# Both expert products and the transposes as two 64-row halves that exchange PSUM banks half way

## The chip, the cores and the metric

One core of a Trainium2 chip. The metric is the device time of one execution in microseconds (us), median of several executions. Everything is fp32. "Faster" and "slower" mean a difference of more than 2%.

## The reference, cut to what matters

Eight sequences of 3584 tokens with 192 channels pass a causal convolution of seven taps (softmaxed weights per head), then a layer of eight experts. Each token goes to one expert, either its own best or, when a locality gate says so, the expert of the token before it:

```python
logits = np.einsum('bsd,de->bse', x, w_gate)
local_gate = 1.0 / (1.0 + np.exp(-np.einsum('bsd,de->bse', x, w_local).squeeze(-1)))
for b in range(B):
    prev_e = -1
    for s in range(S):
        fresh_e = int(np.argmax(logits[b, s]))
        e = fresh_e if s == 0 or local_gate[b, s] < 0.5 else prev_e   # (cut)
        prev_e = e
        # p = softmax(logits[b, s])
        h = np.maximum(x[b, s] @ w1[e], 0.0)      # 192 -> 1024
        out[b, s] = p[e] * (h @ w2[e])            # 1024 -> 192
```

## The kernel before

The kernel convolves and routes the tokens in 16 groups of 14 x 128 and writes each token to a slot of its expert. Slots come in units of 128 tokens. The expert layer then runs over *blocks* of one unit (57 of them) or two units (87) of one expert; routing of later groups is put between the blocks as "side work". The constants: `P = 128`, `D = 192`, `DR = 64` (the rest of 192 over 128), `F = 1024`, `FK = 8` slices of 128 hidden features, `KT = 2` units at most, `BT = 256` tokens.

192 input channels do not fill 128 rows evenly. The first product therefore has eight full-array matmuls (channels 0 to 127), and eight 64-row matmuls for channels 128 to 191, of which two run side by side, one on each half of the rows, in different PSUM banks. So the array changes between 64-row and 128-row mode twice in every block.

```python
# PSUM, 8 banks: bg (2, side work), xps (1), hps (4), yps (1)

def turn(n, xg):                       # the next block's tokens, transposed
    xps = xps_p.tile([P, 2, BT], F32, name="xps")
    for d in range(2):
        for k in range(n):
            nc.tensor.transpose(xps[:, d, k * P:(k + 1) * P],
                                xg[:, k, Y0 + d * P:Y0 + (d + 1) * P], identity=ident)
    xT = tp.tile([P, 2, BT], F32, name="xT")
    nc.vector.tensor_copy(xT[:, :, :n * P], xps[:, :, :n * P])
    return xT

def hidden(n, wb, xT):                 # first product
    # ... hT, hps (four banks), w = slice(0, n * P)
    for half in range(2):
        for j in range(2):
            for row in range(2):
                rows = slice(row * DR, (row + 1) * DR)
                f0 = F + (half * 2 + j) * P
                nc.tensor.matmul(hps[half * 2 + row][:, j, w], lhsT=wb[rows, f0:f0 + P],
                                 rhs=xT[rows, 1, w], start=(j == 0), stop=False,
                                 skip_group_check=True)
    for s in range(FK):
        nc.tensor.matmul(hps[s // 2][:, s % 2, w], lhsT=wb[:, s * P:(s + 1) * P],
                         rhs=xT[:, 0, w], start=False, stop=True, skip_group_check=True)
        if s % 2:
            nc.scalar.activation(hT[:, s - 1:s + 1, w], hps[s // 2][:, :, w], Act.Relu)
    return hT

def output(n, wb, xg, hT):             # second product, scaled by the gate, scattered
    yps = yps_p.tile([P, KT, D], F32, name="yps")
    for k in range(n):
        for m in range(FK):
            nc.tensor.matmul(yps[:, k, :], lhsT=hT[:, m, k * P:(k + 1) * P],
                             rhs=wb[:, WA + m * D:WA + (m + 1) * D],
                             start=(m == 0), stop=(m == FK - 1))
    # ... ScalarE scales yps into o_sb, GpSimd scatters the rows

for i, (_, n, _, _) in enumerate(blocks):
    # ... loads of later blocks
    hT = hidden(n, wbs[i], xT)
    if i + 1 < len(blocks):
        xT = turn(blocks[i + 1][1], xgs[i + 1])
    step(2.1 * n, 1)                   # side work
    output(n, wbs.pop(i), xgs.pop(i), hT)
    step(2.1 * n, n)
```

The next block's transposes stand between the two products. TensorE does them while ScalarE drains the last bank of the first product.

Of the kernel before, what the change touches and what calls it, by code (L numbers as in the profile page):

```python
# [8 lines left out]
F32 = mybir.dt.float32  # L9
I32 = mybir.dt.int32  # L10
Act = mybir.ActivationFunctionType
Alu = mybir.AluOpType
# [5 lines left out]
P = 128  # L18
# [64 lines left out]
def kernel(  # L83
# [19 lines left out]
    op = ctx.enter_context(tc.tile_pool(name="op", bufs=2))  # L103
    bg_p = ctx.enter_context(tc.tile_pool(name="bg_p", bufs=2, space=PSUM))
    xps_p = ctx.enter_context(tc.tile_pool(name="xps_p", bufs=1, space=PSUM))
# [19 lines left out]
    with tc.tile_pool(name="scr", bufs=1) as scr:  # L125
        w = scr.tile([1, H, KC], F32, name="w")
        nc.scalar.dma_start(out=w, in_=weight.rearrange("(o h) k -> o h k", o=1))
        x_in = {0: load_x(0)}
        nc.gpsimd.memset(ones, 1.0)
        any_ = scr.tile([1, 1], F32, name="any_")  # L130
        nc.scalar.activation(any_, ones[:1, :1], Act.Exp)
        make_identity(nc, ident)
        taps(nc, scr, w)
        cps = bg_p.tile([P, GQ * P], F32, name="bg")
        nc.tensor.matmul(cps[:, :H * KC], lhsT=ones[:1, :], rhs=w.rearrange("o h k -> o (h k)"),
                         start=True, stop=True)
        nc.vector.tensor_copy(c.rearrange("p h k -> p (h k)"), cps[:, :H * KC])
# [24 lines left out]
    def conv(g, x_sb, on_pe=(), alone=False):  # L162
# [16 lines left out]
        def others():  # L179
            for i, h in enumerate(on_pe):  # L180
                cps = hps_p.tile([P, 2, BT], F32, name="hps")
                acc = cps.rearrange("p a b -> p (a b)")[:, :NT * GS]
                for k in range(KC):
                    nc.tensor.matmul(acc, lhsT=dg_of(i, k), rhs=chans(h, k),  # L184
                                     start=(k == 0), stop=(k == KC - 1))
                    if k == KC - 1:
                        nc.scalar.copy(cols(h), acc.rearrange("p (t d) -> p t d", d=GS))
                    yield
# [69 lines left out]
    tabi = {}  # L258



    def route(g, alone):
# [8 lines left out]


        yT = yt.tile([P, 3, 4, 2 * P], F32, name="yT")
        for u in range(3):
            for jj in range(0, 4, 2):
                tps = (hps_p.tile([P, 2, BT], F32, name="hps") if alone and u else
                       bg_p.tile([P, 2, 2 * P], F32, name="bg"))
                for j in range(2):
                    for q in range(GQ):
                        t = min(2 * (4 * q + jj + j), NT - 2)  # L280
                        src = (yr[:, t:t + 2, :].rearrange("p t d -> p (t d)") if u == 2
                               else y_sb[:, t + u, Y0:Y0 + P])
                        nc.tensor.transpose(tps[:, j, q * P:(q + 1) * P], src, identity=ident)  # L283
                if alone and g == 0 and jj:
                    nc.vector.tensor_copy(yT[:, u, jj:jj + 2, :], tps)  # L285
                else:
                    nc.scalar.copy(yT[:, u, jj:jj + 2, :], tps)  # L287
            if not alone:
                yield "hop"
        lps = bg_p.tile([P, 2 * P], F32, name="bg")  # L290
        for u in range(3):
# [9 lines left out]
        yield "hop"  # L301
        ltp = bg_p.tile([P, GQ * P], F32, name="bg")
        for q in range(GQ):
            nc.tensor.transpose(ltp[:, q * P:(q + 1) * P], lsb[:, q * P:(q + 1) * P],  # L304
                                identity=ident)
        yield "pe"
        lt = sm.tile([P, NT + 2, E + 1], F32, name="lt")
        nc.vector.tensor_copy(
            lt.rearrange("p (q j u) e -> p q j (u e)", q=GQ, u=2),
            ltp.rearrange("p (q j e) -> p q j e", q=GQ, j=4)[:, :, :, :2 * (E + 1)])  # L310
        yield 0.3
        lg = lt[:, :NT, :E]
# [34 lines left out]

        rps = bg_p.tile([P, GQ * P], F32, name="bg")
        nc.tensor.transpose(rps[:1, :P], run[:, NT - 1:NT], identity=ident)
# [3 lines left out]
        else:  # L353
            nc.vector.memset(so_far[:, 0:1], 0.0)
        yield 0.1
        yield "pe"
        krow = sm.tile([1, P], F32, name="krow")
        nc.vector.tensor_copy(krow, rps[:1, P:2 * P])
        yield 0.2
        nc.vector.tensor_tensor_scan(so_far[:, 1:], krow, rps[:1, :P], so_far[:, 0:1],  # L360
                                     Alu.mult, Alu.add)
        yield 0.4
        yield "hop"
        bps = bg_p.tile([P, GQ * P], F32, name="bg")
        nc.tensor.transpose(bps[:, 0:1], so_far[:, :P], identity=ident[:1, :1])
        rs = sm.tile([P, NT], F32, name="rs")
        nc.vector.tensor_reduce(rs, ex, axis=AX.X, op=Alu.add)
# [5 lines left out]
        yield "pe"  # L373
        before = sm.tile([P, 1], F32, name="before")
        nc.vector.tensor_copy(before, bps[:, 0:1])
        yield 0.2
        nc.vector.tensor_tensor_scan(run, nf, ch, before, Alu.mult, Alu.add)
# [14 lines left out]
        yield "hop"  # L392
        nps = bg_p.tile([P, GQ * P], F32, name="bg")
        nc.tensor.matmul(nps[:, :E], lhsT=tri, rhs=mine, start=True, stop=True)
        nc.tensor.matmul(nps[:, E:2 * E], lhsT=ones, rhs=mine, start=True, stop=True)  # L395
        offs = sm.tile([P, E], F32, name="offs")
        nc.vector.tensor_tensor(offs, base, less, op=Alu.subtract)
# [27 lines left out]
        yield 0.2  # L425
        yield "placed"
        nc.vector.tensor_tensor(base, base, nps[:, E:2 * E], op=Alu.add)
        yield 0.2
        was = g - 1 if g else None
        if ONE[g] > (ONE[was] if g else 0):  # L430
# [143 lines left out]
    def load_rows(i):  # L574
# [16 lines left out]
        return xg  # L591

    def turn(n, xg):

        xps = xps_p.tile([P, 2, BT], F32, name="xps")
        for d in range(2):
            for k in range(n):
                nc.tensor.transpose(xps[:, d, k * P:(k + 1) * P],  # L598
                                    xg[:, k, Y0 + d * P:Y0 + (d + 1) * P], identity=ident)
        xT = tp.tile([P, 2, BT], F32, name="xT")  # L600
        nc.vector.tensor_copy(xT[:, :, :n * P], xps[:, :, :n * P])  # L601
        return xT

    def hidden(n, wb, xT):
        hT = hp.tile([P, FK, BT], F32, name="hT")
        hps = [hps_p.tile([P, 2, BT], F32, name="hps") for q in range(FK // 2)]
        w = slice(0, n * P)


        for half in range(2):  # L610
            for j in range(2):
                for row in range(2):
                    rows = slice(row * DR, (row + 1) * DR)
                    f0 = F + (half * 2 + j) * P
                    nc.tensor.matmul(hps[half * 2 + row][:, j, w], lhsT=wb[rows, f0:f0 + P],  # L615
                                     rhs=xT[rows, 1, w], start=(j == 0), stop=False,
                                     skip_group_check=True)
        for s in range(FK):
            nc.tensor.matmul(hps[s // 2][:, s % 2, w], lhsT=wb[:, s * P:(s + 1) * P],  # L619
                             rhs=xT[:, 0, w], start=False, stop=True, skip_group_check=True)  # L620
            if s % 2:
                nc.scalar.activation(hT[:, s - 1:s + 1, w], hps[s // 2][:, :, w], Act.Relu)  # L622
        return hT

    def output(n, wb, xg, hT):
        yps = yps_p.tile([P, KT, D], F32, name="yps")
        for k in range(n):
            for m in range(FK):
                nc.tensor.matmul(yps[:, k, :], lhsT=hT[:, m, k * P:(k + 1) * P],  # L629
                                 rhs=wb[:, WA + m * D:WA + (m + 1) * D],  # L630
                                 start=(m == 0), stop=(m == FK - 1))
        o_sb = op.tile([P, KT, D], F32, name="o_sb")
        for k in range(n):
            gate = xg[:, k, 0:1]
            nc.scalar.activation(o_sb[:, k, :], yps[:, k, :], Act.Copy, scale=gate)  # L635

# [115 lines left out]
    for i, (_, n, _, _) in enumerate(blocks):  # L752
        ensure(i)
        weights(i + AHEAD)
        hT = hidden(n, wbs[i], xT)
        if i + 1 < len(blocks):
            xT = turn(blocks[i + 1][1], xgs[i + 1])
        step(2.1 * n, 1)
        output(n, wbs.pop(i), xgs.pop(i), hT)
        step(2.1 * n, n)  # L760


def _w1_layout(np, w1):


    rest = w1[:, P:, :].reshape(E, DR, 2, 2, 2, P)
    rest = rest.transpose(0, 3, 1, 2, 4, 5).reshape(E, P, F // 2)
    return np.concatenate([w1[:, :P, :], rest], 2)
# [36 lines left out]
```

## Time and profile before

| before | |
|---|---|
| median of 3 executions | 1467.62 us |
| TensorE busy, granted clock | 98% of the span, full |
| ScalarE, VectorE, GpSimd busy | 35%, 44%, 34% |
| period of a block of two units, no side work beside it | 11.217 us |
| period of a block of one unit, the same | 5.894 us |
| first block starts | 69.7 us |

The *period* is the distance between the starts of the first product in consecutive blocks, late in the run where the routing is finished. 144 blocks with few varieties make up 1312 of 1466 us, so a term of 0.1 us in every block is 14 us, 1%. A timeline row is read as start, duration, engine, line, operation, output and inputs, count, and in brackets how long the engine had been idle and what ended that. The page's lines and two timelines are shown in the prediction below.

### The profile page before, as it was taken

How to read it: one execution, taken by the hardware profiler on the slowest of the kernel's cores; microseconds unless marked ns; L12 is line 12 of the kernel's file. 1: busy time of each engine (PE TensorE's matmuls, PEld its weight loads, DVE VectorE, ACT ScalarE, POOL GpSimd, SP SyncE). 2: the span in 40 equal slices, each digit the busy share in tenths (PEclk: the TensorE clock that was granted, in tenths of full speed). 3: DMA queues.
4: the chain of work that ended last, by engine and by line, in shares of the span. 5: the costliest groups of instructions: out<-in, count | busy, mean ns of one | idle time of the engine just before them, and what ended most of it. 6: DMA issues, size and time to landing. Idle time of an engine off the chain costs nothing.

```text
span 1465.7 us, 25910 instructions
## 1 busy us (share of the span) xinstructions
PE 1434.6 (98%) x9792; PEld 1288.0 (88%) x9792; DVE 650.3 (44%) x1756; ACT 512.9 (35%) x1098; POOL 499.5 (34%) x524
## 2 busy tenths in 40 slices
PE   7799999999999999999999999999999999999998
PEld 4598999989888898888988889889889988999997
DVE  7676766676666666666666664220000000000000
ACT  3244444343343433434334343232222222223332
POOL 1442434334344443444434344344121111112111
PEclk9899999999999999999999999999999999999999
DMA  4499989967475675756757556566555455547883
GB/s 166 137 402 358 341 318 388 337 260 271 171 268 202 241 260 188 254 202 239 260 190 255 201 187 209 187 223 218 174 192 195 167 175 196 188 156 255 299 310 119
DMA packets 66414, 343.01 MB, mean 234 GB/s; under 512 B 12656, under 2 KB 23655, under 8 KB 45810
## 3 DMA queue, kind: packets, MB, share of 16 engines
q1 hardware_dynamic: 44064, 288.66, 55.5%
q0 software_dynamic: 22224, 52.70, 9.3%
q8 instruction: 77, 1.26, 0.3%
q14 instruction: 47, 0.39, 0.1%
q10 hardware_dynamic: 2, 0.00, 0.0%
HBM read 288.51 MB, written 53.49 MB: 233 GB/s over the span
## 4 chain that ended last, share of the span: by engine, by line
PE 61%; issue 29%; POOL 6%; DMA 2%; DVE 1%; POOLq 0%; ACT 0%; SPq 0%; DVEq 0%; ACTq 0%
PE yps L629 25%; PE hps L619 17%; PE hps L615 9%; POOL out_dram L638 5%; PE bg L283 3%; PE xps L598 2%; PE hps L184 2%; PE bg L294 2%; POOL slots L450 2%; DVE y_sb L201 1%; DMA xg<-slots 1%; DMA x_sb<-in_x_dram 1%; POOLq L638 0%; PE bg L304 0%; PE bg L395 0%
## 5 line engine op out<-in xcount | busy, mean ns | idle before, releaser
L629 PE MATMUL yps<-wb,hT 128*128 128x192 f32 x3696 | 625.6, 326 | 0.0
L629 PEld LDWEIGHTS yps<-wb,hT 128*128 128x128 f32 x3696 | 597.2, 190 | 0.2
L638 POOL DMA_INDIRECT out_dram<-o_sb,xg x231 | 240.9, 1043 | 830.1 <-ACT o_sb L635 763.2
L619 PE MATMUL hps<-xT,wb 128*128 128x256 f32 (+1 forms) x2304 | 441.5, 345 | 0.0
L619 PEld LDWEIGHTS hps<-xT,wb 128*128 128x128 f32 x2304 | 364.2, 191 | 67.3 <-issue 29.0
L201 DVE SCALAR_TENSOR_TENSOR y_sb<-x_sb,c,y_sb 128x336 f32<-128x336 f32 x720 | 411.1, 581 | 19.5 <-ACT y_sb L177 2.4
L622 ACT ACTIVATE hT<-hps 128x512 f32<-128x512 f32 (+1 forms) x576 | 295.5, 513 | 344.5 <-PE hps L619 337.4
L601 DVE COPY xT<-xps 128x512 f32<-128x512 f32 (+1 forms) x144 | 84.4, 586 | 739.2 <-PE xps L598 739.2
L635 ACT ACTIVATE o_sb<-yps,xg 128x192 f32<-128x192 f32 x231 | 87.8, 418 | 546.4 <-PE yps L629 544.0
L450 POOL DMA_INDIRECT slots<-y_sb,posi x224 | 219.5, 980 | 110.5 <-issue 89.1
L615 PE MATMUL hps<-xT,wb 64*128 64x256 f32 (+1 forms) x2304 | 240.9, 349 | 1.2 <-DVE y_sb L201 0.7
L615 PEld LDWEIGHTS hps<-xT,wb 64*128 64x128 f32 x2304 | 183.4, 188 | 43.4 <-issue 17.2
L598 PE MATMUL xps<-ident,xg 128*128 128x128 f32 x462 | 74.3, 273 | 4.6 <-DMA xg<-slots 4.6
L598 PEld LDWEIGHTS xps<-ident,xg 128*128 128x128 f32 x462 | 57.9, 142 | 13.7 <-DMA xg<-slots 2.7
L177 ACT ACTIVATE y_sb<-x_sb,c 128x336 f32<-128x336 f32 x116 | 65.9, 579 | 0.4
L287 ACT COPY yT<-bg 128x512 f32<-128x512 f32 x87 | 46.6, 590 | 4.9 <-PE bg L283 4.8
L184 PE MATMUL hps<-x_sb,wb 128*128 128x336 f32 x112 | 34.5, 467 | 3.7 <-DMA x_sb<-in_x_dram 3.7
L184 PEld LDWEIGHTS hps<-x_sb,wb 128*128 128x128 f32 x112 | 21.9, 199 | 14.1 <-issue 5.0
L283 PE MATMUL bg<-ident,y_sb 128*128 128x128 f32 x240 | 31.2, 273 | 1.8 <-DVE y_sb L201 0.7
L283 PEld LDWEIGHTS bg<-ident,y_sb 128*128 128x128 f32 x240 | 27.5, 141 | 3.4 <-issue 1.1
L294 PE MATMUL bg<-yT,wg 128*32 128x256 f32 (+1 forms) x384 | 25.0, 358 | 1.3 <-DVE yT L285 1.3
L294 PEld LDWEIGHTS bg<-yT,wg 128*32 128x32 f32 x384 | 12.3, 109 | 9.7 <-issue 3.3
(139 smaller groups left out, 349.5 us busy)
## 6 DMA issues: line engine op xcount, KB each, us to landing
wb<-in_w_dram SPq DMA_DIRECT2D x144, 1536.0 KB
x_sb<-in_x_dram SPq DMA_DIRECT2D x16, 1920.0 KB
xg<-slots SPq DMA_DIRECT2D x87, 258.0 KB
xg<-slots SPq DMA_DIRECT2D x57, 129.0 KB
out_dram<-o_sb,xg POOLq DMA_INDIRECT x231
slots<-y_sb,posi POOLq DMA_INDIRECT x224
slots<-pad SPq DMA_DIRECT2D x1, 129.0 KB
slots<-pad,toi POOLq DMA_INDIRECT x8
```

What stands on the lines that cost most here:

```text
L184: nc.tensor.matmul(acc, lhsT=dg_of(i, k), rhs=chans(h, k), start=(k == 0), stop=(k == KC - 1))
L201: nc.vector.scalar_tensor_tensor(cols(h), chans(h, k), c[:, h, k:k + 1], cols(h), Alu.mult, Alu.add)
L283: nc.tensor.transpose(tps[:, j, q * P:(q + 1) * P], src, identity=ident)
L450: ins = nc.gpsimd.indirect_dma_start(out=slots[:, :], in_=rows, in_offset=None, out_offset=bass.IndirectOffsetOnAxis(ap=to, axis=0)).ins
L598: nc.tensor.transpose(xps[:, d, k * P:(k + 1) * P], xg[:, k, Y0 + d * P:Y0 + (d + 1) * P], identity=ident)
L601: nc.vector.tensor_copy(xT[:, :, :n * P], xps[:, :, :n * P])
L615: nc.tensor.matmul(hps[half * 2 + row][:, j, w], lhsT=wb[rows, f0:f0 + P], rhs=xT[rows, 1, w], start=(j == 0), stop=False, skip_group_chec ...
L619: nc.tensor.matmul(hps[s // 2][:, s % 2, w], lhsT=wb[:, s * P:(s + 1) * P], rhs=xT[:, 0, w], start=False, stop=True, skip_group_check=True)
L622: nc.scalar.activation(hT[:, s - 1:s + 1, w], hps[s // 2][:, :, w], Act.Relu)
L629: nc.tensor.matmul(yps[:, k, :], lhsT=hT[:, m, k * P:(k + 1) * P], rhs=wb[:, WA + m * D:WA + (m + 1) * D], start=(m == 0), stop=(m == FK - 1))
L635: nc.scalar.activation(o_sb[:, k, :], yps[:, k, :], Act.Copy, scale=gate)
L638: sent = nc.gpsimd.indirect_dma_start(out=out, in_=o_sb[:, k, :], in_offset=None, out_offset=bass.IndirectOffsetOnAxis(ap=xg.bitcast(I32)[ ...
```

## The change

The intent: a 64-row pair takes the slot of one full matmul (0.216 us for 256 columns, the prediction's reading), so if *everything* in a block runs in 64-row mode, the array does not change mode there. Each half takes the rows 0 to 63 or 64 to 127 of the contraction. Two row halves must not write one PSUM bank at once (the prediction names the page that says so), so each works on banks of its own and they exchange banks half way. A sequencer-only instruction on ScalarE ("pass") waits for both halves' last matmuls before the exchange and lets the next ones go. The first product no longer interleaves two kinds of matmuls but runs twelve steps (one matmul on each half, two slots of TensorE time). The second product is cut into two parts, and the next block's transposes move from between the products to between these parts. Only blocks of two units exchange banks in the second product; in a block of one unit each half keeps a bank of its own, and VectorE adds the two results at the end. The two banks that side work had for itself are given to the wider `xps` and `yps`, so side work borrows `hps` banks and has to copy its results out earlier.

```diff
+    def turn_half(to, src, half):
+        rows = slice(half * DR, (half + 1) * DR)
+        nc.tensor.transpose(to, src[rows, :], identity=ident[rows, rows])
 ...
     def turn(n, xg):
-        xps = xps_p.tile([P, 2, BT], F32, name="xps")
+        xps = xps_p.tile([P, 2, 512], F32, name="xps")
 ...        (each transpose becomes two of 64 rows, VectorE puts the halves together)
+    ORDER = [[(0, 0), (1, 0), (0, 1), (1, 1), (2, 0), (3, 0), (2, 1), (3, 1),
+              (4, 0), (5, 0), (6, 0), (7, 0)],
+             [(4, 0), (5, 0), (4, 1), (5, 1), (6, 0), (7, 0), (6, 1), (7, 1),
+              (0, 0), (1, 0), (2, 0), (3, 0)]]
+    def pass_by(last_of):
+        seen = nc.scalar.nop()
+        for half in range(2):
+            tc.add_manual_dep(seen.ins, last_of[half], SYNC, reason="the bank's")
+        return seen
     def hidden(n, wb, xT):
 ...
+        for at in range(len(ORDER[0])):
+            for half in range(2):
+                f, last = ORDER[half][at]
+                rows = slice(half * DR, (half + 1) * DR)
+                f0 = F + f % 4 * P if last else f * P
+                b = f // 2
+                mm = nc.tensor.matmul(hps[b][:, f % 2, w], lhsT=wb[rows, f0:f0 + P],
+                                      rhs=xT[rows, last, w], start=(left[b] == 6),
+                                      stop=(left[b] <= 2), skip_group_check=True)
 ...        (waits for the pass at steps 9 and 11)
+            for half in range(2):
+                f, last = ORDER[half][at]
+                b = f // 2
+                left[b] -= 1
+                if not left[b]:
+                    nc.scalar.activation(hT[:, 2 * b:2 * b + 2, w], hps[b][:, :, w], Act.Relu)
-    def output(n, wb, xg, hT):
+    def output(n, wb, hT, yps, part, done):
+        for m in [0, 1, 4, 5, 2, 3, 6, 7]:
+            if n == 1 and (m % 4 < 2) == part:
+                continue
+            for half in range(2):
+                rows = slice(half * DR, (half + 1) * DR)
+                k = (part + half) % 2 if n == KT else 0
 ...        (one 64-row matmul; two units: part 1 waits for the pass)
 ...
         hT = hidden(n, wbs[i], xT)
+        output(n, wbs[i], hT, yps, 0, done)
         if i + 1 < len(blocks):
             xT = turn(blocks[i + 1][1], xgs[i + 1])
         step(2.1 * n, 1)
-        output(n, wbs.pop(i), xgs.pop(i), hT)
+        output(n, wbs.pop(i), hT, yps, 1, done)
+        send(n, xgs.pop(i), yps)
```

In `ORDER` a pair is (feature slice f, rest-of-channels flag); slice f lies in bank f // 2. `ORDER[0]` is the upper half's list, `ORDER[1]` the lower's. Follow a bank and count its six steps: bank 0 gets four from the upper half (steps 1 to 4) and two from the lower (9, 10); bank 2 the reverse; so 0 and 2 are complete after step 10, and 1 and 3 after step 12.

## The prediction

> **What bounds the kernel now.** I read the page first: engine totals, slices, then the costliest groups.
>
> ```profile
> PE 1434.6 (98%) x9792; PEld 1288.0 (88%) x9792; DVE 650.3 (44%) x1756; ACT 512.9 (35%) x1098; POOL 499.5 (34%) x524
> ...
> PEclk9899999999999999999999999999999999999999
> ...
> L629 PE MATMUL yps<-wb,hT 128*128 128x192 f32 x3696 | 625.6, 326 | 0.0
> ...
> L619 PE MATMUL hps<-xT,wb 128*128 128x256 f32 (+1 forms) x2304 | 441.5, 345 | 0.0
> ...
> L622 ACT ACTIVATE hT<-hps 128x512 f32<-128x512 f32 (+1 forms) x576 | 295.5, 513 | 344.5 <-PE hps L619 337.4
> ...
> L615 PE MATMUL hps<-xT,wb 64*128 64x256 f32 (+1 forms) x2304 | 240.9, 349 | 1.2 <-DVE y_sb L201 0.7
> ...
> L598 PE MATMUL xps<-ident,xg 128*128 128x128 f32 x462 | 74.3, 273 | 4.6 <-DMA xg<-slots 4.6
> ```
>
> TensorE is busy 98% of the span at full clock; its four expert lines take 1382 of 1435 us and wait for almost nothing. ScalarE and VectorE are at 35 and 44%. So the time is TensorE's, and any gain must be TensorE slots saved. (Every f32 matmul stands as two instructions; a transpose as one.)
>
> The second view is the timeline of a block of two units (256 tokens) late in the run, where no side work is left:
>
> ```profile
> 1106.23 2.00 PE L615 MATMUL hps<-xT,wb 64*128 64x256 f32 x16
> ...
> 1108.15 3.72 PE L619 MATMUL hps<-xT,wb 128*128 128x256 f32 x16
> 1109.38 0.60 ACT L622 ACTIVATE hT<-hps 128x512 f32<-128x512 f32 x1 [2.31 <-PE hps L619]
> 1110.18 0.60 ACT L622 ACTIVATE hT<-hps 128x512 f32<-128x512 f32 x1 [0.21 <-PE hps L619]
> 1111.05 0.60 ACT L622 ACTIVATE hT<-hps 128x512 f32<-128x512 f32 x1 [0.27 <-PE hps L619]
> ...
> 1111.71 0.60 PE L598 MATMUL xps<-ident,xg 128*128 128x128 f32 x4
> 1111.91 0.60 ACT L622 ACTIVATE hT<-hps 128x512 f32<-128x512 f32 x1 [0.27 <-PE hps L619]
> ...
> 1112.15 5.37 PE L629 MATMUL yps<-wb,hT 128*128 128x192 f32 x32
> ...
> 1117.44 1.60 PEld L615 LDWEIGHTS hps<-xT,wb 64*128 64x128 f32 x16 [0.23 <-issue]
> 1117.44 2.00 PE L615 MATMUL hps<-xT,wb 64*128 64x256 f32 x16
> ```
>
> The period is 11.22 us, the same for 29 such blocks in a row. Steady starts inside a phase lie 0.216 us apart for 256 columns (a pair of 64-row matmuls, which start 7 ns apart, also takes 0.216), 0.1626 for 192 and 0.109 for a transpose. Then 8 pairs x 0.216 = 1.73, 16 x 0.216 = 3.46, 4 x 0.109 = 0.44, 32 x 0.1626 = 5.20: sum 10.82. The missing 0.39 us lies in two places, where the array goes from 128 rows to 64 (1112.15 to 1117.44 is 5.29, not 5.20, and the first pair after it takes 0.320 instead of 0.216) and back (about 0.20 each). Also note that ScalarE drains the first product while it still runs: four evictions, each beginning as a bank completes, the last beside the next block's transposes.
>
> The same view for a block of one unit:
>
> ```profile
> 1331.45 2.05 PE L619 MATMUL hps<-xT,wb 128*128 128x128 f32 x16
> 1332.26 1.66 ACT L622 ACTIVATE hT<-hps 128x256 f32<-128x256 f32 x4 [1.06 <-PE hps L619]
> ...
> 1333.34 0.38 PE L598 MATMUL xps<-ident,xg 128*128 128x128 f32 x2
> ...
> 1333.56 2.77 PE L629 MATMUL yps<-wb,hT 128*128 128x192 f32 x16
> ...
> 1336.25 1.16 PE L615 MATMUL hps<-xT,wb 64*128 64x128 f32 x16
> ```
>
> Period 5.894 us: 24 slots x 0.1117 + 16 x 0.1626 + 2 x 0.109 = 5.50, and again 0.40 for two switches. There are 87 blocks of two units and 57 of one (counts of the xg loads), so 87 x 11.217 + 57 x 5.894 = 1312 us; 70 us pass before the first block, and the remaining 84 us are side work (routing of later groups) put between blocks, 5.17 us a group in the steady part.
>
> **What the Trainium skill says.** "TensorEngine Tiling (Array Packing)", section "Key Properties": changing the tiling mode drains TensorE, while tiles of one mode run independently. The trace agrees: some 0.2 us a switch, two a block, and pairs 7 ns apart. "PSUM — Partial Sum Buffer", section "PSUM bank collisions raise a hardware error": two row tiles may not write one bank at a time, and software must see to it. Hence the exchange of banks; no run yet shows its price. "TensorE: Matmul & The Clock Gate", section "LDWEIGHTS": a load costs its columns at 1.2 GHz (107 ns for 128), whatever the rows. The trace agrees: matmuls with 8 moving columns behind 128-column loads still come 0.112 us apart. A weight load of a transpose, however, lasts 142 ns against 190 for others, so a transpose of half the rows may come faster than 0.109 us a pair.
>
> **The change, part by part.**
>
> (a) Switches. All expert matmuls become 64-row pairs. A pair takes a full matmul's slot, so the slots stay 24 and 32 (24 and 16), and both switches go: -0.39 us x 87 and -0.40 x 57 = -57 us. That is the intent.
>
> (b) Transposes. The two halves move 64 columns instead of 128. If the pair is bound by the 57 ns that a transpose's load takes beyond its fixed 84, estimate 0.064 us a pair instead of 0.109; if by issue or a full load, no gain. Up to -0.18 us a two-unit block, but see (d).
>
> (c) The wait for the evictions, which I take to decide it. Each half begins in banks of its own, and all four banks complete only in the last four of the twelve steps: banks 0 and 2 together after step 10, banks 1 and 3 after step 12. The second product now follows at once; the transposes no longer stand between. By the order of the built instructions, its first matmul waits for the *second* eviction (bank 2 is drained first, the product begins with bank 0). From the start T of the last matmuls of step 10, two units: the eviction begins at T+0.475 (1109.38 less 1108.91, the start of the fourth matmul of L619), the second ends one back-to-back interval later (0.49, from four copies of 512 columns in a row in the opening): T+0.475+0.598+0.49 = 1.56. A ScalarE result lets a weight load start 0.052 us later (seen where the logits are transposed), and the first load without prefetch costs 0.104 more, as at the switches: T+1.72. TensorE arrives at T+5x0.216 = 1.08. Stall 0.64 us. One unit: T+0.372+0.281+0.384+0.156 = 1.19 against 5x0.1117 = 0.56: stall 0.635 us.
>
> (d) The exchange in the second product (two units only). The halves swap columns' banks only after ScalarE has seen the first part end; meanwhile the next transposes run. Matmul end 0.333, ScalarE's pass some 0.065, back to a load 0.05, unprefetched load 0.104: 0.55 after the last start, less its own slot 0.163 = 0.39 us, against 0.26 to 0.44 of transposes. So transposes plus exchange cost 0.39 to 0.44, as the transposes alone do today. The exchange inside the first product has 0.5 us or more of slack and costs nothing.
>
> Bare blocks: two units 24x0.216 + 0.64 + 5.20 + 0.41 = 11.44 (+0.22); one unit 2.68 + 0.635 + 2.60 + 0.13 to 0.22 = 6.09 (+0.20). Over all: 87 x 0.22 + 57 x 0.20 = +31 us.
>
> (e) Side work. Its transposes may gain up to 26 x 0.045 = 1.2 us a group, but the two small full-array groups (carries, counts) now stand alone in 64-row surroundings and pay two switches each, +0.4, the logits and the single-row transpose +0.2 each: about zero to +0.7 us a group. Borrowed banks must be copied out by ScalarE before the first product takes them. They are allotted last, so I see a wait of about 0.3 us only with one-unit blocks. Together +3 us for 14 groups, with the opening.
>
> Sum: 1467.6 + 31 + 3 = about 1501 us.
>
> **Rivals.** First, the intent holds: the evictions hide, the switches go, transposes shorten: 1467.6 - 57 - up to 20 = 1390 to 1410. For it: the 0.39 us a block is real and all engines but TensorE have spare time. Against it: spare share doesn't help when both evictions start within one step of the end; 1.2 us of ScalarE work cannot fit in the 0.86 us of the last two steps. Second, the stall equals the gain: were the first load's 0.104 hidden and the transposes at 0.064 in one-unit blocks, the bare blocks come out at +0.10 and +0.05, giving about 1480. Third, worse: side work on ScalarE (0.48 us a copy or scaling) stands ahead of an eviction or a pass, each delaying TensorE, or the sequencer cannot feed twice the instructions: 1520 to 1540. Against the last: the L615 phase of one-unit blocks sustains four instructions in 0.112 us. Memory is no rival: weights are prefetched three blocks ahead and blocks grow longer.
>
> **Range and chances.** Switch savings and the eviction stall rest on measured intervals (0.05 us of error each, 7 us over 144 blocks); half transposes and side work add some 10. So 1501, range 1480 to 1524. The 2% line is 1497, inside the range but below the middle: slower by over 2% 0.60, within 0.34, faster 0.06.
>
> **What would show it.** Right: late two-unit blocks with a period near 11.44 and one-unit blocks near 6.09; TensorE's weight load of the second product idle about 0.6 us a block with ScalarE's eviction as releaser, and evictions in back-to-back couples at the end of the first product; no 0.32 us first pairs between products. Wrong: no wait for hT, or periods under 11.0 and 5.6 (then the matmuls' real ends are earlier than I read them); or the loss lying in groups with side work alone; or pairs of 192 columns slower than 0.163 us.

## The result, and the profile after

The changed kernel takes 1494.6 us (median, 1494.31 to 1494.98), against 1467.65 of the kernel before beside it: ratio 1.0182, with a 95% interval of 1.0164 to 1.02. It is 1.8% slower, which the 2% rule calls the same (in a second set below, the interval touches 1.02 and the rule says unclear). (Ratios here are the mean time of one kernel's fast runs over that of the other's of the same rounds, so not quite the ratio of the medians quoted.) The result is correct, and the clock was full but for stretches of the opening and the last 3 us.

The changed kernel's page, costliest groups (busy time, mean ns of one, then idle time before them and what ended it):

```profile
PE 1408.2 (94%) x16670; PEld 1272.2 (85%) x16670; DVE 649.0 (43%) x1773; ACT 479.9 (32%) x1168; POOL 500.9 (34%) x524
...
L681 PE MATMUL yps<-wb,hT 64*128 64x192 f32 x7392 | 672.4, 330 | 52.2 <-ACT hT L671 52.2
L681 PEld LDWEIGHTS yps<-wb,hT 64*128 64x128 f32 x7392 | 594.9, 187 | 99.6 <-ACT hT L671 98.1
...
L671 ACT ACTIVATE hT<-hps 128x512 f32<-128x512 f32 (+1 forms) x576 | 248.8, 519 | 422.6 <-PE hps L658 422.6
...
L264 PEld LDWEIGHTS xps<-ident,xg 64*128 64x128 f32 x924 | 52.6, 139 | 2.9 <-DMA xg<-slots 0.3
L264 PE MATMUL xps<-ident,xg 64*128 64x64 f32 x924 | 52.2, 221 | 0.2 <-DMA xg<-slots 0.2
```

TensorE now does *less* busy time (1408 us against 1435) in a longer span. The difference is in the last columns: before, the second product had waited 0.0 us for matmuls and 0.2 for weight loads; now its weight loads wait 98.1 us for ScalarE's evictions. The view of waits counts 144 of them, one for each block, 0.68 us each:

```profile
PEld yps L681 <- ACT hT L671: 98.1, 144, 1.1
```

The timeline of two late blocks of two units:

```profile
1153.32 2.87 PE L681 MATMUL yps<-wb,hT 64*128 64x192 f32 x32 [0.37 <-ACT hT L671]
...
1156.03 0.41 PE L264 MATMUL xps<-ident,xg 64*128 64x64 f32 x8
...
1156.31 2.87 PE L681 MATMUL yps<-wb,hT 64*128 64x192 f32 x32
...
1159.01 5.35 PE L658 MATMUL hps<-xT,wb 64*128 64x256 f32 x48
...
1163.59 2.06 ACT L671 ACTIVATE hT<-hps 128x512 f32<-128x512 f32 x4 [3.63 <-PE hps L658]
1164.72 2.58 PEld L681 LDWEIGHTS yps<-wb,hT 64*128 64x128 f32 x32 [0.77 <-ACT hT L671]
1164.72 2.87 PE L681 MATMUL yps<-wb,hT 64*128 64x192 f32 x32 [0.37 <-ACT hT L671]
```

The period is 1164.72 less 1153.32, 11.40 us. Take it apart by starts:

| stretch | starts | measured | work at full pace | lost |
|---|---|---|---|---|
| first product | 1159.01 to 1164.72 | 5.71 | 24 x 0.216 = 5.18 | 0.53 |
| second product, part one | 1153.32 to 1156.03 | 2.71 | 16 x 0.1626 = 2.60 | 0.11 |
| transposes | 1156.03 to 1156.31 | 0.28 | 4 x 0.063 = 0.25 | 0.03 |
| second product, part two | 1156.31 to 1159.01 | 2.70 | 2.60 | 0.10 |

The four evictions, which before began one by one while the first product ran, are now one row of ScalarE of four back to back: it begins 4.58 us into the product and lasts until after the second product would have started. The second product starts 1.13 us after the first eviction does, which is two evictions (one interval of 0.49 and one duration of 0.60) and a hand-over of 0.05. (The 0.063 is the median distance of pairs of half transposes in this trace. The 0.03 and the 0.10 after it I put down to the exchange; blocks of one unit, which have none, lose 0.06 at that place.) The 0.37 us in TensorE's bracket is smaller than the 0.53 lost between starts, because it counts from the matmuls' modelled ends.

A late block of one unit, same view:

```profile
1401.85 2.84 PE L658 MATMUL hps<-xT,wb 64*128 64x128 f32 x48
...
1404.34 1.21 ACT L671 ACTIVATE hT<-hps 128x256 f32<-128x256 f32 x4 [1.86 <-PE hps L658]
1405.05 1.57 PE L681 MATMUL yps<-wb,hT 64*128 64x192 f32 x16 [0.36 <-ACT hT L671]
...
1406.45 0.29 PE L264 MATMUL xps<-ident,xg 64*128 64x64 f32 x4
...
1407.93 2.85 PE L658 MATMUL hps<-xT,wb 64*128 64x128 f32 x48
```

Its period is 6.08 us: 0.52 us are lost before the second product (3.20 against 24 x 0.1117 = 2.68), and its first part takes 1.40 instead of 1.30.

Where the 27.5 us between the two profiled spans (1493.2 and 1465.7) are:

| | us |
|---|---|
| 87 blocks of two units x (11.405 - 11.217) | +16.4 |
| 57 blocks of one unit x (6.083 - 5.894) | +10.8 |
| first block starts at 73.4 instead of 69.7 us | +3.7 |
| rest: side work between blocks and the end | -3.4 |

The sums of the actual distances between block starts say where the -3.4 lies: the blocks of two units take 15.3 us more than before and not 16.4, those of one unit 7.8 and not 10.8, and from the last block's start to the end it is 0.8 us more. So blocks that have side work beside them pay less for the change than bare ones. (A steady group of five two-unit blocks with side work costs about 5.0 to 5.1 us more than five bare ones; it was 5.17 before.)

The opening is longer for at least two reasons, which no run separates. Its convolution matmuls now write the wide `xps` and `yps` tiles, of which two matmul groups share one, and TensorE waits 0.53 us for ScalarE five times there, once before. And the granted clock was at half from 34.7 to 41.5 us and for 13.7 us from 65.4 on, before only for 10.2 us from 63.3 on; in the first of these stretches six convolution matmuls took 3.73 us instead of 1.86.

### The profile page after: what moved, and what is told of

It is laid out like the page before. It is cut to its first block, busy times and chain, and to the rows that moved or that the text cites. A ratio compares the mean times of both kernels' runs of the same rounds, so it can differ in the third digit from the quotient of the medians.

```text
span 1493.2 us, 40292 instructions
## 1 busy us (share of the span) xinstructions
PE 1408.2 (94%) x16670; PEld 1272.2 (85%) x16670; DVE 649.0 (43%) x1773; ACT 479.9 (32%) x1168; POOL 500.9 (34%) x524
## 4 chain that ended last, share of the span: by engine, by line
PE 54%; issue 30%; ACT 6%; POOL 6%; DVE 3%; DMA 0%; POOLq 0%; DVEq 0%; ACTq 0%
PE yps L681 25%; PE hps L658 22%; ACT hT L671 5%; POOL out_dram L702 5%; PE hps L264 2%; PE hps L308 2%; PE yps L185 1%; POOL slots L467 1%; PE xps L264 1%; PE xps L185 1%; DVE y_sb L202 1%; DMA x_sb<-in_x_dram 0%; DVE xT L624 0%; PE hps L407 0%; POOLq L702 0%
## 5 line engine op out<-in xcount | busy, mean ns | idle before, releaser
L681 PE MATMUL yps<-wb,hT 64*128 64x192 f32 x7392 | 672.4, 330 | 52.2 <-ACT hT L671 52.2
L681 PEld LDWEIGHTS yps<-wb,hT 64*128 64x128 f32 x7392 | 594.9, 187 | 99.6 <-ACT hT L671 98.1
L658 PE MATMUL hps<-xT,wb 64*128 64x256 f32 (+1 forms) x6912 | 636.5, 337 | 1.2 <-DVE xT L627 1.2
L658 PEld LDWEIGHTS hps<-xT,wb 64*128 64x128 f32 x6912 | 563.0, 188 | 51.9 <-DVE y_sb L202 3.7
L671 ACT ACTIVATE hT<-hps 128x512 f32<-128x512 f32 (+1 forms) x576 | 248.8, 519 | 422.6 <-PE hps L658 422.6
L624 DVE COPY xT<-xps 128x512 f32<-128x512 f32 x87 | 60.2, 692 | 592.9 <-PE xps L264 592.9
L301 ACT COPY yT<-hps 128x512 f32<-128x512 f32 x93 | 49.8, 592 | 44.5 <-PE hps L264 44.4
L264 PEld LDWEIGHTS xps<-ident,xg 64*128 64x128 f32 x924 | 52.6, 139 | 2.9 <-DMA xg<-slots 0.3
L264 PE MATMUL xps<-ident,xg 64*128 64x64 f32 x924 | 52.2, 221 | 0.2 <-DMA xg<-slots 0.2
L308 PE MATMUL hps<-yT,wg 128*32 128x256 f32 (+1 forms) x384 | 25.1, 367 | 2.4 <-issue 2.1
```

Source lines behind the costliest of these rows:

```text
L264: nc.tensor.transpose(to, src[rows, :], identity=ident[rows, rows])
L308: nc.tensor.matmul(lps[32 * j:32 * j + 32, :w], lhsT=wg[:, u, :], rhs=yT[:, u, j, :w], start=(u == 0), stop=(u == 2))
L624: nc.vector.tensor_copy(to.rearrange("p h d k s -> p h (d k) s"), xps[:, :, :BT].rearrange("p h (x s) -> p h x s", s=DR))
L658: mm = nc.tensor.matmul(hps[b][:, f % 2, w], lhsT=wb[rows, f0:f0 + P], rhs=xT[rows, last, w], start=(left[b] == 6), stop=(left[b] <= 2), s ...
L671: nc.scalar.activation(hT[:, 2 * b:2 * b + 2, w], hps[b][:, :, w], Act.Relu)
L681: mm = nc.tensor.matmul(yps[:, half if n == 1 else k, :D], lhsT=hT[rows, m, k * P:(k + 1) * P], rhs=wb[rows, WA + m * D:WA + (m + 1) * D], ...
```

## The experiments

Twelve runs of eight kernels were made, in three sets: the first on one chip, the second and third on another. The letters are those of the expectations. Three theories at the start, and two that were added:

- **W (the evictions).** The change saves the switches (0.40 us a block), and gives back more, because two evictions must end between the completion of banks 0 and 2 and the start of the second product. Then an edit that drains in the right order, or completes banks earlier, takes off computable amounts.
- **X (the exchanges)** of banks by way of ScalarE cost the time, and **Y (the pairs themselves)**: half matmuls come slower, or twice the instructions cannot be fed. Under both, the wait for `hT` is only where the cost shows; such edits leave the time at 1494 us or raise it.
- **V (the chip, added after the first set).** That chip, or the state it was in, makes TensorE's semaphore updates late. Its rival **Z**: the edits themselves do.

### Set one, on a slower chip

Four edits of the changed kernel. **e1** lets the second product begin with bank 2, which ScalarE drains first:

```diff
-        for m in [0, 1, 4, 5, 2, 3, 6, 7]:
+        for m in [4, 5, 0, 1, 6, 7, 2, 3]:
 ...
-                                      start=(m == 0 and not part),
-                                      stop=(m == FK - 1 and part == 1), skip_group_check=True)
-                if n == KT and part and m == 0:
+                                      start=(m == 4 and not part),
+                                      stop=(m == 3 and part == 1), skip_group_check=True)
+                if n == KT and part and m == 4:
```

> Only the order in which the second product takes its blocks of hidden units changes: it begins with bank 2, which ScalarE drains first, instead of bank 0. Theory W (the first matmul waits for two evictions in a row): the wait shrinks by the second eviction's interval, 0.49 us with two units and 0.28 with one, to about 0.15 and 0.35 us. Periods 10.92 and 5.80, in all 87 x 0.49 + 57 x 0.28 = 59 us less than the changed kernel: 1436 us. Rival X (the exchange of banks, which goes through ScalarE, is what costs): nothing changes, 1494. Rival Y (half matmuls come slower, or twice the instructions cannot be fed): nothing changes either, 1494.

**e2** leaves the second product alone, and orders the first so that banks 0 and 2 are complete after step 8 of 12 instead of 10:

```diff
-    ORDER = [[(0, 0), (1, 0), (0, 1), (1, 1), (2, 0), (3, 0), (2, 1), (3, 1),
-              (4, 0), (5, 0), (6, 0), (7, 0)],
-             [(4, 0), (5, 0), (4, 1), (5, 1), (6, 0), (7, 0), (6, 1), (7, 1),
-              (0, 0), (1, 0), (2, 0), (3, 0)]]
+    ORDER = [[(0, 0), (1, 0), (0, 1), (1, 1), (6, 0), (7, 0), (4, 0), (5, 0),
+              (2, 0), (3, 0), (2, 1), (3, 1)],
+             [(4, 0), (5, 0), (4, 1), (5, 1), (2, 0), (3, 0), (0, 0), (1, 0),
+              (6, 0), (7, 0), (6, 1), (7, 1)]]
 ...
-            if at in (3, 7):
-                passed[8 if at == 3 else 10] = pass_by(last_of)
+            if at in (3, 5):
+                passed[6 if at == 3 else 8] = pass_by(last_of)
```

> Only the first product's order changes: each half now does 4 steps on its first bank, 2 on the other half's second bank, 2 on the other half's first bank, 4 on its second bank. Banks 0 and 2 are complete after step 8 instead of 10, four steps before the end; the slack of both exchanges is two steps. The second product still begins with bank 0, drained second. Theory W: no wait with two units (eviction done 1.72 us after the start of step 8's last matmuls, TensorE there after 1.94), 0.19 us left with one unit (1.19 against 1.00). Periods 10.77 and 5.64: 87 x 0.64 + 57 x 0.445 = 81 us less, 1414 us. Rival X: the exchanges have less slack than before (one had four steps), so the time rises above 1494. Rival Y: 1494.

**e3** is e2 with the second product in the order in which that first product's banks are drained, `for m in [4, 5, 0, 1, 2, 3, 6, 7]` (flags and wait moved as in e1, with the stop at m == 7).

> Both orders together; the second product takes banks 2, 0, 1, 3, as they are drained. Theory W: no wait for evictions at all, periods 11.405 - 0.64 = 10.77 and 6.083 - 0.635 = 5.45: 87 x 0.64 + 57 x 0.635 = 92 us less than the changed kernel, 1403 us, which is 4.4% faster than the kernel before. Rivals X and Y: 1494 or more.

**e4** puts the next block's transposes back between the products, where they stood before the change:

```diff
-        output(n, wbs[i], hT, yps, 0, done)
         if i + 1 < len(blocks):
             xT = turn(blocks[i + 1][1], xgs[i + 1])
+        output(n, wbs[i], hT, yps, 0, done)
```

> The next block's transposes stand before the second product again, as in the kernel before, instead of between its halves. Theory W: they vanish into the wait for the evictions (0.63 us, transposes 0.28 with two units and 0.12 with one), but the exchange between the halves, which they covered, stands open at 0.39 us. Two units: from 0.63 + 0.28 + 0.10 to 0.64 + 0.39, period 11.42 (+0.02); one unit, which has no exchange there: 6.083 - 0.12 = 5.96. In all 5 us less, 1490 us. Rival X (the exchange is the main cost): with nothing beside it the exchange costs more and nothing is won back, two units 11.7 or more, 1515 us or more. Rival Y: 1494.

Measured, against 1481.18 us of the kernel before on the same chip:

| | us | ratio to before (95%) |
|---|---|---|
| e1 | 1538.66 | 1.0369 (1.0339 to 1.0398) |
| e2 | 1517.65 | 1.0239 (1.0207 to 1.0272) |
| e3 | 1504.9 | 1.0155 (1.0138 to 1.0172) |
| e4 | 1571.09 | 1.0594 (1.0575 to 1.0614) |

All results were correct, and all four times are far off what W expected. At face value they speak against W: what should have removed a wait made the kernel slower. But the late blocks without side work were just where W had put them: e3 at 10.763 us (two units) and 5.455, e1 at 10.916, e4 at 11.405 for two units. (The one-unit blocks of e1 and e4 were off, at 6.04 to 6.12 and 6.16 to 6.21.) The time was lost elsewhere: before the first block, which starts at 82.4 to 83.2 us (71.2 to 73.4 in the same kernels on the other chip), in the passes of the first product (e1's weight loads there waited 37.6 us for them, on the other chip not once), and in ScalarE's evictions, which began late. From e3's timeline on this chip:

```profile
1057.17 1.08 ACT L671 ACTIVATE hT<-hps 128x512 f32<-128x512 f32 x2 [2.81 <-PE hps L658]
...
1060.00 1.30 ACT L671 ACTIVATE hT<-hps 128x512 f32<-128x512 f32 x2 [1.74 <-PE hps L658]
```

The second couple begins 2.83 us after the first; in a quiet block of the same program (its timeline is shown below) it begins 1.66 us after. In the trace I compared the moment of each update of TensorE's semaphore with the modelled end of its matmul. On this chip some 450 to 475 of some 1480 updates in each of the four kernels came more than 60 ns late, the last percentile of them by 2.4 to 3.4 us. (The count takes the next recorded update after each matmul; 28 to 54 updates are missing from these traces, so a small part of it may be gaps in the record. And as a matmul's end is modelled, a late update cannot be told from a late matmul.) In all the other traces 16 to 23 did. The kernel before was itself 0.9% slower here than elsewhere. This gave theory V, with Z as its rival; two more sets were run on another chip, with copies of both kernels among them.

### Set two: the same kernels on another chip

**b** is the kernel before, and **a** the changed kernel, both unedited, beside e3 again.

> The kernel before, unchanged, for a trace of it on the same chip as the experiments. The first four experiments ran on a chip on which the kernel before took 1481 us instead of 1468, and in their traces about 450 of TensorE's semaphore updates came 0.1 to 5 us late, while those of before and of the changed kernel on the first chip had none but the 16 at other engines' hand-offs. Theory V (that chip or its state delays semaphore updates in stretches with side work; kernels with more hand-offs suffer more): on a chip of that kind 1481 us with late updates as well, on the other kind 1468 us without.

> The changed kernel, unchanged. Theory V on a slow chip: side-free blocks again 11.405 and 6.083, the time well above 1494, about 1540 to 1590 (near the fourth experiment, 1571, or the first, 1539), for it hands over to ScalarE and back as often. On a chip like the first: 1494.6. Rival Z (the experiments' edits made the late updates, not the chip): 1494.6 and no late updates on any chip.

> The kernel with both orders, unchanged, beside the two others on one chip. Theory W with V: on a chip like the first 1403 us; on a slow chip 1505 us again, but 80 to 92 us or more below the changed kernel there. Rival Z: 1505 us on either chip, slower than the changed kernel.

**e5** asks what the switches are worth, in the kernel *before*. Its 64-row pairs become single full-row matmuls of the same slots. The contraction is then wrong (the output is off by 0.54 in relative error); data flow, evictions and the count of slots stay; the count of instructions in these slots halves, and only banks 0 and 2 receive this part.

```diff
             for j in range(2):
-                for row in range(2):
-                    rows = slice(row * DR, (row + 1) * DR)
-                    f0 = F + (half * 2 + j) * P
-                    nc.tensor.matmul(hps[half * 2 + row][:, j, w], lhsT=wb[rows, f0:f0 + P],
-                                     rhs=xT[rows, 1, w], start=(j == 0), stop=False,
-                                     skip_group_check=True)
+                f0 = F + (half * 2 + j) * P
+                nc.tensor.matmul(hps[half * 2][:, j, w], lhsT=wb[:, f0:f0 + P],
+                                 rhs=xT[:, 1, w], start=(j == 0), stop=False,
+                                 skip_group_check=True)
 ...
-                             rhs=xT[:, 0, w], start=False, stop=True, skip_group_check=True)
+                             rhs=xT[:, 0, w], start=(s % 4 == 2), stop=True, skip_group_check=True)
```

> Wrong results on purpose: the kernel before, but its 64-row pairs are issued as full 128-row matmuls of the same count of slots, which add two halves that do not belong together. So the two changes of tiling mode go and nothing else (no exchange, no half transposes). Step (a) of the prediction: periods 11.217 - 0.39 = 10.82 and 5.894 - 0.40 = 5.49, in all 57 us less than the kernel before, 1410 us on a chip like the first. Were the switches not the cause of the missing 0.39 us, periods 11.2 and 5.9 and no gain.

| | us | ratio to before (95%) | two-unit period | one-unit period |
|---|---|---|---|---|
| b | 1467.07 (one run) | | 11.217 | 5.894 |
| a | 1494.65 | 1.0183 (1.0166 to 1.02) | 11.405 | 6.083 |
| e3 | 1407.89 | 0.9595 (0.9579 to 0.9611) | 10.763 | 5.454 |
| e5 | 1418.7 | 0.9668 (0.9652 to 0.9684) | 10.819 | 5.498 |

The changed kernel repeats its time to 0.05 us. e3, the same program that had lost on the first chip, is 4.05% faster than before and correct: Z is refuted. The first set's times belong to that chip, or to the state it was in. X and Y are refuted as well: e3 issues as many TensorE instructions as the changed kernel (16670) and makes the same exchanges, and is 86.8 us faster.

In e5 the switches are worth 0.398 us in a block of two units and 0.396 in one of one. Its timeline:

```profile
1100.53 5.37 PE L627 MATMUL yps<-wb,hT 128*128 128x192 f32 x32
...
1105.74 1.89 PE L613 MATMUL hps<-xT,wb 128*128 128x256 f32 x8
...
1107.46 3.62 PE L617 MATMUL hps<-xT,wb 128*128 128x256 f32 x16
...
1110.92 0.60 PE L598 MATMUL xps<-ident,xg 128*128 128x128 f32 x4
```

1100.53 to 1105.74 is 5.21 us, where the kernel before had 5.29, and 1105.74 to 1107.46 is 1.72, where it had 1.92 (1106.23 to 1108.15): both the drain towards 64 rows and the one back have gone. The whole run gains 49 us, not 57. Part of the missing 8 was found: early one-unit blocks are 4.6 us slower than their saving allows, and where side work changes the mode anyway a block keeps its switch (a steady group of five blocks took 59.57 us where the periods gave 59.27).

e3's timeline shows what W wanted to see:

```profile
1110.60 1.08 ACT L671 ACTIVATE hT<-hps 128x512 f32<-128x512 f32 x2 [2.77 <-PE hps L658]
...
1112.06 2.77 PE L681 MATMUL yps<-wb,hT 64*128 64x192 f32 x32
1112.26 1.08 ACT L671 ACTIVATE hT<-hps 128x512 f32<-128x512 f32 x2 [0.58 <-PE hps L658]
...
1114.94 2.87 PE L681 MATMUL yps<-wb,hT 64*128 64x192 f32 x32
```

The evictions now stand as two couples. The first ends at 1111.68, before the second product begins at 1112.06, and no releaser stands in brackets behind it. The second couple runs *beside* the second product, which needs its result only some 1.3 us later. Compared with the changed kernel, the whole 0.64 and 0.63 us a block are gone. Over all blocks that is 0.642 x 87 + 0.629 x 57 = 91.7 us; 86.8 arrived. The other 5 were given back in the early one-unit blocks, where a faster TensorE now catches up with other things: one of them stands 2.59 us waiting for its expert's weights, a transfer from memory.

### Set three: each edit alone, and another engine

On a chip without late updates, the single edits again:

> The first experiment once more (only the second product's order: bank 2 first), because its chip was of the slow kind. Theory W on a chip on which the kernel before takes 1468: periods 10.92 and 5.80, 1436 us, a few us more where early blocks meet other limits (the kernel with both orders ended 5 us above its estimate). Rivals X and Y (exchange, or half matmuls as such): 1494.

> The second experiment once more (only the first product's order: banks 0 and 2 complete four steps before the end). Theory W: periods 10.77 and 5.64, 1414 to 1419 us. Rival X: above 1494, since the exchanges have less slack. Rival Y: 1494.

> The fourth experiment once more (the next block's transposes before the second product, inside the wait). Theory W: two-unit period 11.42 (11.405 was seen on the slow chip), one-unit 5.96, 1490 us. Side work that stood between the halves still does. Rival X: 1515 us or more.

**e6** attacks the wait without a change of order: bank 0's eviction, the second of the couple, goes to VectorE, so that both run at once.

```diff
-                    nc.scalar.activation(hT[:, 2 * b:2 * b + 2, w], hps[b][:, :, w], Act.Relu)
+                    if b == 0:
+                        nc.vector.tensor_scalar(hT[:, 2 * b:2 * b + 2, w], hps[b][:, :, w],
+                                                0.0, None, Alu.max)
+                    else:
+                        nc.scalar.activation(hT[:, 2 * b:2 * b + 2, w], hps[b][:, :, w], Act.Relu)
```

> The changed kernel with one edit: the eviction of bank 0, the second of the couple that the second product waits for, is done by VectorE (a maximum with zero) while ScalarE does bank 2. Orders stay. Theory W: both end about 0.69 us (two units, as VectorE's copy of 512 columns) or 0.42 us after they begin, so the wait falls from 0.64 to 0.24 and from 0.635 to 0.39 us where VectorE is free: periods 11.00 and 5.84. In all 87 x 0.40 + 57 x 0.245 = 49 us less, 1446 us, if VectorE were always free; in blocks with side work a 0.58 us operation of VectorE may be in the way, so 1446 to 1480. Rivals X and Y: 1494.

| | us | ratio to before (95%) | two-unit period | one-unit period |
|---|---|---|---|---|
| e1 | 1437.77 | 0.9797 (0.9781 to 0.9813) | 10.916 | 5.808 |
| e2 | 1416.44 | 0.965 (0.9634 to 0.9666) | 10.764 | 5.637 |
| e4 | 1474.16 | 1.0042 (1.0026 to 1.0059) | 11.405 | 5.909 |
| e6 | 1503.7 | 1.0244 (1.0219 to 1.0268) | 11.131 | 5.89 |

By the 2% rule e1 is unclear, as its interval holds 0.98, e2 faster, e4 the same and e6 slower; all four differ clearly from the changed kernel's 1494.65 us on this chip.

**e1 and e2** came as W expected. e1's gain over the changed kernel is 0.489 us (two units) and 0.275 (one): the interval of one eviction in each (the rows of four above give (2.06 - 0.60)/3 = 0.49 for two units and, with one eviction of 0.385, (1.21 - 0.385)/3 = 0.275 for one). So the product did wait for the second eviction of the couple, and now waits for the first. The weight loads' wait for `hT` falls from 98.1 to 39.8 us:

```profile
PEld yps L681 <- ACT hT L671: 39.8, 140, 0.6
```

e2 takes away the whole wait of two-unit blocks, and of one-unit blocks 0.446 of 0.629, the rest coming only with e3's order. Under X or Y neither should have lowered the time at all.

**e4** beat its expectation: 20.5 us less than the changed kernel. The late blocks of two units did not move, as expected: 0.28 us of transposes go into the wait and come back as an uncovered exchange.

```profile
1159.77 2.58 PEld L681 LDWEIGHTS yps<-wb,hT 64*128 64x128 f32 x32 [0.27 <-ACT hT L671]
...
1162.75 0.30 PEld L681 LDWEIGHTS yps<-wb,hT 64*128 64x128 f32 x4 [0.41 <-ACTq L640]
```

The wait for `hT` has fallen from 0.77 to 0.27 us, and a new one of 0.41 has come for ScalarE's sequencer, which is the pass of the exchange. Blocks of one unit have no such exchange and gain 0.174 where they are bare; by the sums of the periods all 57 together gain 8.0 us. Those of two units gain 12.9 (a steady group of five takes 60.79 us here, 62.0 to 62.1 in the changed kernel), which I had valued at zero. The view of waits shows why:

```profile
PEld yps L681 <- ACTq L640: 18.2, 45, 0.4
```

The exchange stands open in about half of the 87 blocks only. In the 43 others TensorE has side work between the two parts, which covers the exchange, so there the transposes do vanish into the wait.

**e6** failed, and its expectation with it. Late blocks gained only 0.274 and 0.193 us; VectorE's hand-over to the weight load took 0.12 us where I had put ScalarE's 0.052. In blocks with side work it is a loss:

```profile
605.65 3.43 DVE L202 SCALAR_TENSOR_TENSOR y_sb<-x_sb,c,y_sb 128x336 f32<-128x336 f32 x6
...
608.23 0.60 ACT L675 ACTIVATE hT<-hps 128x512 f32<-128x512 f32 x1 [3.58 <-PE hps L658]
609.00 0.68 DVE L672 TENSOR_SCALAR hT<-hps 128x512 f32<-128x512 f32 x1
609.73 2.87 PE L685 MATMUL yps<-wb,hT 64*128 64x192 f32 x32 [0.74 <-DVE hT L672]
```

ScalarE takes its bank at 608.23. VectorE takes the other, complete at the same time, at 609.00, because six convolution steps stand ahead of it in order (605.65 to 609.08 by their count and length). TensorE waits for it until 609.73. VectorE is 49% busy in e6, but what counts is the queue in front of this one instruction. TensorE's matmuls waited 48.4 us for this eviction in all, up to 2.9 us at a time.

## Why the prediction was right or wrong

It put 1501 us, with 1480 to 1524; 1494.6 came. The mechanism and the size were right. The wait before the second product, summed over the starts of all 144 blocks of the changed kernel's trace, is 75 us, and the slow first pair after it adds 0.10 us a block, 15 us; the prediction's stalls, which include that pair, come to 92. The likeliest class in it, slower by over 2%, was not: 1.8% came, 0.2 points under the line.

- **(a) Switches.** The step gave 0.39 and 0.40 us a block; e5 shows 0.398 and 0.396. Right as a saving in a bare block. As a sum over all blocks (57 us) it is an upper bound: e5's whole run gained 49.
- **(b) Half transposes.** Estimated at 0.064 us a pair. Measured: 0.063 from pair to pair, against 0.109 of a full transpose. Right, and the alternative "no gain" is out.
- **(c) The wait for the evictions.** 0.64 us in two-unit blocks: measured 0.53 + 0.11 between starts. 0.635 in one-unit blocks: measured 0.52 + 0.10. e1, e2 and e3 show the parts of it: the second eviction's interval, and the late completion of the banks. This step carried the prediction, and it holds. One detail differs: the evictions stand in one row of four, not in couples, as the second couple's banks are complete before the first couple is drained.
- **(d) The exchange.** 0.39 us for transposes and exchange together; measured 0.28 + 0.10 = 0.38. Right, and e4 shows the other side: without the transposes over it, the exchange costs 0.38 us between starts (0.41 as idle time of the weight load).
- **Bare blocks.** 11.44 and 6.09 against 11.405 and 6.083, so 27.2 us for the 31 predicted.
- **(e) Side work and the opening.** This is the mis-sized term: +3 us predicted; +3.7 (opening) and -3.4 (the rest) measured, so +0.3 in sum. That these two, neither of them foreseen at that size, all but cancelled is luck. The likely reason for the -3.4, argued and not shown, is the one that e4 and e5 make plausible: a block with side work is not a bare block plus side work. Some of the switches and of the exchange lie under it.
- **The rivals.** The first (1390 to 1410) describes e3, that is, this change with its evictions hidden. The second put 1480 if the load and transposes came cheaper; the 0.10 of the load was not hidden (0.11 and 0.10 lost in part one). The third (instruction feeding, ScalarE's queue) is hardly seen in the changed kernel's trace: in two of the 87 two-unit blocks the wait before the second product is 0.81 us instead of 0.53. But its form, side work ahead of an eviction, is what sank e6 on VectorE.

The two errors, some 4 us in the bare blocks and 3 us in side work, have the same sign, and their sum moved the result across the 2% line. A forecast with its centre 4 us above a class boundary and errors of that size should not have given 0.60 to the one side.

What stays open: why one chip's traces have some 450 late updates of TensorE's semaphore, whether these are the cause of its longer times or only go with it, and what the changed kernel would take there; no trace of it or of the kernel before was taken on that chip. All four edits lost nearly the same there, 97 to 101 us against their runs on the other chip, so they rank alike on both; by the same shift the changed kernel would take some 1592 to 1596 us there (an estimate, not run), while the kernel before lost only 14. The granted clock explains little of it: it was at half for 50 to 58 us of these four runs, on the other chip for some 20, which is about 19 us of work lost at most.

## What to carry to other kernels

The slots saved on the saturated engine counted only once the engine that drains it finished in time: let the first banks complete well before the end of a product (here four steps of twelve), and let the next product consume them in the order in which they are drained. e3 did this with two lists of numbers, and turned a change that lost 1.8% into one that gains 4% over the kernel before. When an edit's result contradicts its own quiet stretches in the trace, run the unchanged kernels beside it on another chip before you give up the theory.

## What the Trainium skill lacked or had wrong

- "TensorEngine Tiling (Array Packing)", section "Key Properties", says that a change of tiling mode drains TensorE and gives no price. Here two changes cost 0.396 to 0.398 us together (e5).
- "PSUM — Partial Sum Buffer", section "PSUM bank collisions raise a hardware error", leaves it to software to keep two row tiles out of one bank, without a price. Here an exchange by way of ScalarE's sequencer left 0.10 us beside 0.28 us of transposes, and 0.41 us of weight-load idle with nothing beside it (e4).
- "TensorE: Matmul & The Clock Gate", section "LDWEIGHTS", gives columns / 1.2 ns, which is 107 ns for 128, and makes no exception. Full transposes came every 109 ns, but pairs of half transposes, each half with a load of 128 columns, every 63. Loads of 107 ns would not allow that even side by side on the two row halves. In the records a half transpose's load lasts 139 ns against 187 for other loads, so it is probably quicker; no run shows why.
- No page was found on updates of TensorE's semaphore that come late on one chip: some 450 to 475 of some 1480 there were over 60 ns late, against 16 to 23 elsewhere, and the same program took 1504.9 us instead of 1407.9.
- No page was found on what VectorE's hand-over to a weight load takes: 0.12 us in e6, against 0.05 of ScalarE.
